# An attention stage whose block-mean rows are made in place by a product and a ScalarE copy

## The chip, the cores and the metric

One core of a Trainium2 chip runs the kernel. The metric is the device time of one execution in microseconds (us); the number to move is the median of several runs. The engines are named as in the profile: PE is TensorE, ACT is ScalarE, DVE is VectorE, POOL is GpSimd, SP is SyncE, whose queue issues nearly all transfers here.

## What is computed

Attention over 2 x 8 heads of 768 positions and 64 dimensions, and behind it two dense gated layers. Every query sees its neighbours within 15 positions and 24 rows that each stand for a block of 32 keys: the block's maximum on the key side, the block's mean on the value side.

```python
nb = S // block                                             # 768 // 32 = 24
k_sum = k.reshape(B, H, nb, block, D).max(axis=3)
v_sum = v.reshape(B, H, nb, block, D).mean(axis=3)
scores_l = scale * np.matmul(q, k.transpose(0, 1, 3, 2))    # kept where |i - j| < 16
scores_s = scale * np.einsum('bhsd,bhnd->bhsn', q, k_sum) + np.log(block)
a = softmax(np.concatenate([scores_l_m, scores_s], axis=-1))
out = np.matmul(a, np.concatenate([v, v_sum], axis=2))
# then: h = x @ w_in; x = (h * cos(h)) @ w_out; and once more with h * tanh(softplus(h))
```

## The kernel before

The attention runs over 8 pairs of heads. A pair has six tiles of 128 queries, so there are 48 steps, numbered 0 to 47: step i is tile i mod 6 of pair i // 6. Everything is in float32.

A step is one pass of the loop at the end of `attention`. It handles several tiles at once, at different stages: the scores of tile i (`scores`), the exponentials of tile i - 1 (`softmax1`), the normalising of tile i - 3 (`softmax2`), the transposes of the probabilities of tile i - 5 (`probsT`) and the product with the values of tile i - 6 (`pv`). The work is collected in lists by phase (`at`), and `flush` issues them in the order of `ORDER`. So on PE a step reads: two score products (`bank<-kx,qt`), three transposes of probabilities (`bank<-ident,pn`), the preparation of a later pair (transposes `ident,kn` or `ident,qn`), and the product of probabilities and values, in two parts: `pt,vn` for the 128 positions of the tile itself, then `pt,vt` for the tail. The accumulators of `pv` are banks 6 and 7 in turn, two steps each. After each flush `filler` adds the early work on the dense layers' weights (L106 the load, L130 and L172/L174 on ACT, L135, L144 and L179 on DVE).

The tail tile `vt` holds, for each of the six tiles of a pair, the rows that are not in the tile: 15 neighbour rows on each side and the 24 block means, for two heads, 108 rows in all. Three such tiles rotate (`VT[n % 3]`). The neighbour rows are loaded from DRAM by `load_v`. The block means come in two ways:

- Pairs 0 to 2: PE makes them from the values by a product with `means` (`prep_vm`, in step 6n + 3, for pair 0 in step 4), ACT copies them to the tile `vm`, and `prep_vs` has SP send them to their rows of `vt` by two transfers, each repeated over the six tiles.
- Pairs 3 to 7: POOL adds up the 32 rows of each block in `vb` in nine instructions (`block_sums`, steps 14 to 21 and 26 to 33), scales the sum into `vs` (120 partitions, one for each block of five heads), and `prep_vs` sends 24 partitions for each head to `vt`.

On POOL a step's own work is the normalising: one instruction for the tile's own 128 columns, and for the tail one of 108 columns where the tile is even and two of 60 and 48 columns where it is odd. SP works its queue in order: a transfer that waits, for its source or for room, holds up all behind it.

## Time and profile before

| | us |
|---|---|
| median of 3 runs (617.55 to 620.34) | 619.26 |
| the profiled execution | 620.15 |
| its span, first to last instruction | 618.4 |
| PE busy in the span | 605.7 |
| ACT, DVE, POOL busy | 393.8, 457.6, 173.5 |
| mean granted TensorE clock | 0.992 of full |

The rows further down come from the same execution. A timeline row gives the start, the time from the first start to the last end, the engine, the line, the operation with output and inputs, and the count of instructions; in brackets stand the idle time ahead of it and what ended that. A matmul in float32 is two instructions, so "x4" is two products. [...]

### The profile page before, as it was taken

What the parts mean: (1) busy time and instruction counts of PE and PEld (TensorE: products, weight loads), DVE (VectorE), ACT (ScalarE), POOL (GpSimd) and SP (SyncE); (2) the same over time, 40 slices, a digit from 0 to 9 for tenths busy, and PEclk for the clock granted to TensorE, in tenths of its full rate; (3) what the DMA queues carried; (4) which work ended last, traced back from release to release, by engine and by line L of the source; (5) the groups of instructions that cost most, each with busy time, mean ns of one, the idle gap of its engine ahead of it and who ended that gap; (6) DMA issues with size and microseconds to landing.
All of it is one profiled execution on the core that took longest, in us unless ns stands there. A gap on an engine that the chain in (4) does not pass through costs nothing.

```text
span 618.4 us, 9241 instructions
## 1 busy us (share of the span) xinstructions
PE 605.7 (98%) x3212; PEld 505.9 (82%) x3212; DVE 457.6 (74%) x952; ACT 393.8 (64%) x849; POOL 173.5 (28%) x261
## 2 busy tenths in 40 slices
PE   8989899999999999999999999999999999999998
PEld 4768688888888788888888878888888888888886
DVE  6638677488767786868686898977878786968544
ACT  6749789786558777766767769765454545444331
POOL 6538846653612542323232470000000000000000
PEclk9979999999999999999999999999999999999999
DMA  8886941302012212212211221142221222221004
GB/s 185 165 201 148 205 120 40 103 1 69 1 36 100 71 68 69 70 68 69 68 69 69 69 69 33 36 137 68 69 68 69 69 68 103 68 69 36 0 35 170
DMA packets 58842, 49.90 MB, mean 81 GB/s; under 512 B 44396, under 2 KB 44652, under 8 KB 58796
## 3 DMA queue, kind: packets, MB, share of 16 engines
q1 hardware_dynamic: 57708, 49.06, 27.2%
q8 instruction: 25, 0.41, 0.3%
q10 hardware_dynamic: 1088, 0.26, 0.2%
q14 instruction: 21, 0.17, 0.1%
HBM read 45.57 MB, written 3.15 MB: 79 GB/s over the span
## 4 chain that ended last, share of the span: by engine, by line
PE 92%; DMA 3%; DVE 2%; POOL 1%; SPq 1%; issue 1%; ACT 0%; ACTq 0%; POOLq 0%
PE bank L729 33%; PE bank L920 21%; PE bank L907 14%; PE bank L285 13%; PE bank L213 5%; PE bank L621 5%; DMA vt<-vs 1%; DMA qn<-in_q_dram 1%; POOL wx L193 1%; DVE gl L628 1%; POOL pn L285 1%; DVE acc L628 0%; DMA kn<-in_k_dram 0%; DMA vt<-vm 0%; DVE ws L179 0%
## 5 line engine op out<-in xcount | busy, mean ns | idle before, releaser
L729 PE MATMUL bank<-xh,ws 128*128 128x512 f32 (+1 forms) x464 | 133.5, 345 | 0.0
L920 PE MATMUL bank<-ws,gh 128*128 128x512 f32 (+1 forms) x388 | 119.2, 389 | 0.0
L628 DVE TENSOR_TENSOR acc<-acc,bank 128x512 f32<-128x512 f32 (+1 forms) x133 | 90.0, 681 | 35.0 <-PE bank L920 25.9
L907 PE MATMUL bank<-gh,ws 128*128 128x512 f32 x288 | 95.7, 390 | 0.0
L729 PEld LDWEIGHTS bank<-xh,ws 128*128 128x128 f32 x464 | 83.3, 189 | 12.2
L920 PEld LDWEIGHTS bank<-ws,gh 128*128 128x128 f32 x388 | 70.9, 188 | 13.0
L729 PE MATMUL bank<-xl,ws 128*128 128x512 f32 (+1 forms) x232 | 80.1, 345 | 0.0
L920 PE MATMUL bank<-ws,gl 128*128 128x512 f32 (+1 forms) x194 | 75.0, 387 | 0.0
L907 PEld LDWEIGHTS bank<-gh,ws 128*128 128x128 f32 x288 | 54.2, 188 | 10.8
L628 DVE TENSOR_TENSOR gl<-gg,gh 128x512 fp32r<-128x512 f32 x78 | 56.3, 735 | 8.4 <-ACT gh L882 8.0
L285 POOL TENSOR_TENSOR pn<-pb,rs 128x256 f32<-128x256 f32 (+3 forms) x120 | 51.5, 452 | 38.9 <-DVE rs L285 14.7
L172 ACT CAST ws<-wx 128x512 fp32r<-128x512 f32 (+1 forms) x62 | 36.3, 597 | 39.7 <-DVE wx L156 20.7
L882 ACT CAST gh<-gg 128x512 fp32r<-128x512 f32 x96 | 58.3, 618 | 3.2 <-DVE gg L874 2.2
L729 PE MATMUL bank<-ws,ws 128*128 128x512 f32 (+1 forms) x300 | 56.9, 338 | 0.3 <-DVE ws L179 0.3
L907 PE MATMUL bank<-gl,ws 128*128 128x512 f32 x144 | 56.4, 392 | 0.1
L729 PEld LDWEIGHTS bank<-ws,ws 128*128 128x128 f32 x300 | 48.1, 189 | 7.8 <-DVE ws L179 0.7
L285 DVE CUSTOM_DVE_ANT_0 pb<-bank,mask 128x182 f32<-128x182 f32 x96 | 29.5, 344 | 28.9 <-PE bank L285 23.2
L729 PEld LDWEIGHTS bank<-xl,ws 128*128 128x128 f32 x232 | 43.8, 189 | 6.7
L867 DVE SCALAR_TENSOR_TENSOR gg<-gg,bank 128x512 f32<-128x512 int32 x36 | 24.2, 684 | 27.2 <-ACT gg L864 27.2
L920 PEld LDWEIGHTS bank<-ws,gl 128*128 128x128 f32 x194 | 36.4, 188 | 7.7
L285 ACT ACTIVATE pb<-pb,mx 128x182 f32<-128x182 f32 x96 | 42.4, 449 | 0.2 <-DVE mx L285 0.2
L628 POOL TENSOR_TENSOR gl<-gg,gh 128x512 fp32r<-128x512 f32 x18 | 24.1, 1336 | 62.3 <-ACT gh L882 60.0
(146 smaller groups left out, 1188.2 us busy)
## 6 DMA issues: line engine op xcount, KB each, us to landing
wst<-in_moe_w_in_dram SPq DMA_DIRECT2D x32, 512.0 KB, 3.6
wst<-in_moe_w_out_dram SPq DMA_DIRECT2D x32, 512.0 KB, 3.3
vn<-in_v_dram SPq DMA_DIRECT2D x16, 192.0 KB, 3.7
out_dram<-acc SPq DMA_DIRECT2D x11, 256.0 KB, 2.0
kn<-in_k_dram SPq DMA_DIRECT2D x14, 192.0 KB, 3.8
qn<-in_q_dram SPq DMA_DIRECT2D x14, 192.0 KB, 4.2
vb<-in_v_dram SPq DMA_DIRECT2D x4, 480.0 KB
vt<-in_v_dram SPq DMA_DIRECT2D x32, 18.8 KB, 3.1
```

What stands on the lines that cost most here:

```text
L172: nc.scalar.copy(hi, x)
L193: (nc.vector if l else nc.gpsimd).tensor_tensor(out=z, in0=u, in1=v, op=op)
L213: nc.tensor.matmul(ps, lhsT=SLOT[4 * (g % 2) + a][:, 512 * c + 128 * f:512 * c + 128 * f + 128], rhs=X[e][:, c, TB * j:TB * j + TB], start ...
L285: todo[phase].append(lambda: fn(*a, **kw))
L621: nc.tensor.matmul(ps, lhsT=x, rhs=y, start=(n == 0), stop=(n == len(mm) - 1))
L628: (eng or nc.vector).tensor_tensor(out=out, in0=x, in1=y, op=op)
L729: nc.tensor.matmul(ps, lhsT=u, rhs=v, start=start and n == 0, stop=stop and n == len(mm) - 1, skip_group_check=True)
L867: nc.vector.scalar_tensor_tensor(out=x["r"], in0=x["r"].bitcast(I32), scalar=-1.0, in1=src(), op0=ALU.mult, op1=ALU.add)
L882: nc.scalar.copy(slot[0], x["r"])
L907: nc.tensor.matmul(BANK[bank], lhsT=x, rhs=y, start=(n == 0 and (h == HF or not stay)), stop=(n == len(mm) - 1 and (h == NH - 1 or not stay)))
L920: nc.tensor.matmul(BANK[bank][:, 0:d1 - d0], lhsT=x, rhs=y, start=(n == 0 and (h == 0 or not stay)), stop=(n == len(mm) - 1 and (h == NH - ...
```

## The change

`vt` gets another order of rows: 32 for the means of the first head (24 used), 32 for the second, then the four groups of 15 neighbour rows, 124 in all. `prep_vm` now makes the means of a pair at these partitions in PSUM for all pairs: for pairs 0 to 2 by the product with `means`, which has 64 columns now, for pairs 3 to 7 by one product (two for pair 5) with a selection matrix `pick` from the block sums; the factor 1/32 is in `pick`. Two ACT copies (`spread`) write the rows straight from PSUM into the six tiles, one for each head: one at the end of step 6n + 3, one at the start of step 6n + 4. `vm`, the transfers `vt<-vm` and `vt<-vs` and the scaling on POOL are gone. The block sums start two steps earlier (steps 12 to 19 and 24 to 31). The normalised tiles `pn` are four fixed tiles, and the tail is normalised by two instructions in every step.

```diff
-            BLOCKS = {a + c: [(g, c)] for g, a in ((0, 14), (1, 26)) for c in range(7)}
+            BLOCKS = {a + c: [(g, c)] for g, a in ((0, 12), (1, 24)) for c in range(7)}
...
+            def build_pick():
+                nc.gpsimd.memset(pick, 0.0)
+                nc.gpsimd.affine_select(
+                    out=pick, in_=pick, pattern=[[-NB, HPG + 2], [-1, MROW]], compare_op=ALU.not_equal,
+                    fill=1.0 / BLK, base=NB, channel_multiplier=1)
+                nc.gpsimd.memset(pick[:, :, NB:MROW], 0.0)
...
-                at("misc", nc.gpsimd.tensor_tensor, out=x[:, r:r + n, :], in0=x[:, r:r + n, :],
-                   in1=x[:, r + w:r + w + n, :], op=ALU.add)
-                if c == 8:
-                    at("misc", nc.gpsimd.tensor_scalar, out=VS[g], in0=x[:, 0, :], scalar1=1.0 / BLK, scalar2=None,
-                       op0=ALU.mult)
+                at("misc", nc.gpsimd.tensor_tensor, out=x[:, r:r + n, :] if c < 8 else VS[g][:, None, :],
+                   in0=x[:, r:r + n, :], in1=x[:, r + w:r + w + n, :], op=ALU.add)
...
-                ps = BANK[6 if n == 1 else 7][0:NB, 0:128]
...
-                vm = VM[n] = p2.tile([NB, 2 * D], F32, tag="vm", name="vm")
-                at("ev", nc.scalar.copy, vm, ps)
-
-            def prep_vs(n):
...
-                    at("misc", nc.sync.dma_start, out=VT[n % 3][r0:r0 + NB, :, e, :],
-                       in_=x[:, None, :].to_broadcast([NB, NTILE, D]))
+                ps = BANK[6 if n % 2 else 7][0:2 * MROW, 0:128]
+                if 2 * n < MADE:
+                    for t in range(NTILE):
+                        at(phase, nc.tensor.matmul, ps, lhsT=means[:, t].rearrange("p e j -> p (e j)"),
+                           rhs=VN[n % 3][:, t, 0:3:2, :], start=(t == 0), stop=(t == NTILE - 1))
+                else:
+                    ps = ps[:, 0:D]
+                    g, c = divmod(2 * n - MADE, HPG)
+                    mm = [(g, c + 1)] + [(g + 1, 0)] * (c == HPG - 1)
+                    for m, (g, c) in enumerate(mm):
+                        at(phase, nc.tensor.matmul, ps, lhsT=pick[:, c:c + 2].rearrange("p e j -> p (e j)"), rhs=VS[g],
+                           start=(m == 0), stop=(m == len(mm) - 1))
+                VM[n] = ps if 2 * n < MADE else None, ps
+
+            def spread(n, e, phase):
+                made, ps = VM[n]
+                x = ps[MROW * e:MROW * e + MROW, D * e if made is not None else 0:][:, 0:D]
+                at(phase, nc.scalar.copy, VT[n % 3][MROW * e:MROW * e + MROW, :, e, :],
+                   x[:, None, :].to_broadcast([MROW, NTILE, D]))
...
-                9: [lambda n: prep_vm(n), lambda n: prep_vs(n)],
+                9: [lambda n: prep_vm(n), lambda n: spread(n, 0, "misc")],
+                10: [lambda n: spread(n, 1, "xh")],
...
-                if STEPS[i][1] % 2 == 0:
-                    norm(0, SIDE, SIDE, 0, 128 + SIDE)
-                else:
-                    norm(0, REST - HALO, HALO, 0, EXT - HALO)
-                    norm(SIDE, -GAP, GAP, HALO, 128 + GAP)
+                odd = STEPS[i][1] % 2
+                norm(2 * MROW, 2 * HALO, HALO, HALO, 0, EXT - HALO)
+                norm(GAP * odd, MROW, -GAP if odd else GAP, GAP, HALO, 128 + GAP)
```

What follows are rows of the instruction order of the two kernels, in which a name ends with a running number. On SP, ahead of the first weight load of the dense layers (`wst`), before:

```order
L319 DMA vt_113<-in_v_dram 15x5x64
L298 DMA qn<-in_q_dram 128x6x64 x2
L285 DMA vt_112<-vm 24x6x64 x2
L298 DMA kn<-in_k_dram 128x6x64 x2
L106 DMA wst<-in_moe_w_in_dram 128x512
```

and now:

```order
L327 DMA vt_113<-in_v_dram 15x5x64
L330 DMA vt_113<-in_v_dram 15x5x64
L309 DMA qn<-in_q_dram 128x6x64 x2
L309 DMA kn<-in_k_dram 128x6x64 x2
L106 DMA wst<-in_moe_w_in_dram 128x512
```

The two transfers with the means of pair 1 are gone from between the loads; nothing else moved on this queue.

On ACT, steps 27 and 28 (pair 4), before; `pt` is the copy of transposed probabilities that ends a step, `ws` is weight work:

```order
L285 COPY pt_1020<-bank5_63 128x384
L174 ACTIVATE ws0_85<-wx_929 128x512
L285 CAST xh_93<-bank6_64 128x256
L285 ACTIVATE pb_1023,sm_1022<-pb_1023,mx_1024 128x182 x2
L285 COPY pt_1051<-bank5_63 128x384
```

and now:

```order
L296 COPY pt_1017<-bank5_63 128x384
L296 COPY vt1_112<-bank7_65 32x6x64
L174 ACTIVATE ws0_85<-wx_927 128x512
L296 COPY vt1_112<-bank7_65 32x6x64
L296 CAST xh_93<-bank6_64 128x256
L296 ACTIVATE pb_1020,sm_1019<-pb_1020,mx_1021 128x182 x2
L296 COPY pt_1048<-bank5_63 128x384
```

The two copies into `vt` stand on both sides of the weight work, ahead of the exponentials of step 28.

On PE, steps 21 and 22 (pair 3), from the last transposes of probabilities in step 21 to the value product of step 22, before, with what an instruction waits for in brackets:

```order
L285 MATMUL bank5_63<-ident_116,pn_770 108x128 [waits Pool_49]
L285 MATMUL bank4_62<-ident_116,qn_542 128x128 [waits DMAHW2_49,DMAHW1_49]
L285 MATMUL bank4_62<-ident_116,qn_542 128x128
L285 MATMUL bank7_65<-pt_800,vn2_110 128x128 x2
L285 MATMUL bank7_65<-pt_800,vt2_113 128x128
...
L285 MATMUL bank6_64<-pt_832,vn2_110 128x128 x2
L285 MATMUL bank6_64<-pt_832,vt2_113 128x128
```

and now:

```order
L296 MATMUL bank5_63<-ident_116,pn0_120 124x128 [waits Pool_49]
L296 MATMUL bank6_64<-vs0_114,pick_119 64x64 [waits DVE_49,Pool_49]
L296 MATMUL bank4_62<-ident_116,qn_548 128x128 [waits DMAHW6_49,DMAHW5_49]
L296 MATMUL bank4_62<-ident_116,qn_548 128x128
L296 MATMUL bank7_65<-pt_802,vn2_110 128x128 x2
L296 MATMUL bank7_65<-pt_802,vt2_113 128x128
...
L296 MATMUL bank6_64<-pt_832,vn2_110 128x128 [waits Activation_49]
L296 MATMUL bank6_64<-pt_832,vn2_110 128x128
L296 MATMUL bank6_64<-pt_832,vt2_113 128x128
```

The new product waits for POOL (the sums in `vs`) and writes bank 6, which the value product of step 22 takes next; that one now waits for ACT, for the second copy out of that bank.

## Rows read from the trace of the kernel before

**Rows 1.** Timeline of PE, steps 11 to 17, the `pt,vt` products alone.
```profile
27.74 0.39 PE L285 MATMUL bank<-pt,vt 108*128 108x128 f32 x2
...
33.49 0.77 PE L285 MATMUL bank<-pt,vt 108*128 108x128 f32 x2 [3.71 <-DMA vt<-vm]
...
39.77 0.39 PE L285 MATMUL bank<-pt,vt 108*128 108x128 f32 x2
...
45.09 0.39 PE L285 MATMUL bank<-pt,vt 108*128 108x128 f32 x2
...
46.97 0.39 PE L285 MATMUL bank<-pt,vt 108*128 108x128 f32 x2
```

**Rows 2.** Timeline of PE: q transposes of step 21, `pt,vt` of steps 23 and 25.
```profile
53.80 0.38 PE L285 MATMUL bank<-ident,qn 128*128 128x128 f32 x2
...
58.22 0.39 PE L285 MATMUL bank<-pt,vt 108*128 108x128 f32 x2
...
62.41 0.39 PE L285 MATMUL bank<-pt,vt 108*128 108x128 f32 x2
```

**Rows 3.** Timeline of PE, `pt,vt` of steps 29, 30 and 32.
```profile
69.91 0.39 PE L285 MATMUL bank<-pt,vt 108*128 108x128 f32 x2
...
74.86 0.46 PE L285 MATMUL bank<-pt,vt 108*128 108x128 f32 x2 [2.92 <-DMA vt<-vs]
...
80.24 0.39 PE L285 MATMUL bank<-pt,vt 108*128 108x128 f32 x2
```

**Rows 4.** Windows: behind the two waits, six steps from 18, the dense layers.
```profile
33.49:39.77 6.28, 6.28 (x30) 5.03 (x31) 1.97 (x11) 2.24 (x8) 0.00 (x0) 0.57 1.00 244
74.86:80.24 5.38, 5.38 (x30) 4.42 (x31) 2.43 (x12) 2.31 (x9) 2.23 (x5) 0.68 0.91 235
47.29:58.54 11.25, 11.25 (x92) 9.28 (x91) 9.36 (x43) 10.53 (x39) 9.76 (x23) 1.00 0.69 164
200.00:618.00 418.00, 414.93 (x2067) 352.40 (x2065) 319.65 (x520) 248.74 (x443) 67.11 (x57) 1.00 0.21 70
```

**Rows 5.** Timeline of SP's queue: issues around the first wait.
```profile
30.31 1.69 SPq L285 DMA_DIRECT2D vt<-vm  x2
...
33.20 0.54 SPq L106 DMA_DIRECT2D wst<-in_moe_w_in_dram  x1
```

**Rows 6.** Timeline of PE, step 15: the product with `means`.
```profile
41.08 1.49 PE L285 MATMUL bank<-vn,means 128*24 128x128 f32 x12
```

**Rows 7.** Groups by form, ACT, 0 to 108 us (count, busy us, mean ns, idle before).
```profile
L285 ACT COPY pt<-bank 128x384 f32<-128x384 f32 x43 | 20.6, 479 | 3.4 <-PE bank L285 3.0
```

**Rows 8.** Timeline of ACT, end of step 45 and start of step 46.
```profile
103.56 0.48 ACT L285 COPY pt<-bank 128x384 f32<-128x384 f32 x1 [0.23 <-PE bank L285]
103.94 0.62 ACT L172 CAST ws<-wx 128x512 fp32r<-128x512 f32 x1
104.45 0.38 ACT L285 CAST xh<-bank 128x256 fp32r<-128x256 f32 x1
```

**Rows 9.** Timeline of PE, step 46: the value product.
```profile
104.96 0.61 PE L285 MATMUL bank<-pt,vn 128*128 128x128 f32 x4
```

**Rows 10.** Groups by form, POOL, 0 to 115 us: normalising of the tail.
```profile
L285 POOL TENSOR_TENSOR pn<-pb,rs 128x108 f32<-128x108 f32 x24 | 8.9, 369 | 0.0
L285 POOL TENSOR_TENSOR pn<-pb,rs 128x60 f32<-128x60 f32 x24 | 8.3, 344 | 0.0
L285 POOL TENSOR_TENSOR pn<-pb,rs 128x48 f32<-128x48 f32 x24 | 6.6, 273 | 1.9
```

**Rows 11.** Timeline of POOL: scaling of the first sums, two instructions of the second.
```profile
55.98 0.37 POOL L285 TENSOR_SCALAR vs<-vb 120x64 f32<-120x64 f32 x1
...
68.26 0.72 POOL L285 TENSOR_TENSOR vb<-vb 120x256 f32<-120x256 f32 x1
...
70.29 1.18 POOL L285 TENSOR_TENSOR vb<-vb 120x256 f32<-120x256 f32 x1
```

**Rows 12.** Timeline of DVE, step 14: first touch of the first weight load.
```profile
39.96 0.42 DVE L135 TENSOR_SCALAR wst<-wst 128x512 int32<-128x512 int32 x1
```

More of the change, by code (lines that the diff above doesn't have):

```diff
@@ L218 @@
     HPG = 5
+    MROW = 32
+    TAIL = 2 * MROW + 4 * HALO
     MADE = B * H - 2 * HPG
@@ L234, in attention @@
             mask = p1.tile([128, 3, EXT], F32, tag="mask", name="mask")
-            means = p1.tile([128, NTILE, NB], F32, tag="means", name="means")
+            means = p1.tile([128, NTILE, 2, MROW], F32, tag="means", name="means")
+            pick = p1.tile([HPG * NB, HPG + 2, MROW], F32, tag="pick", name="pick")
+            PN = [p1.tile([128, 256 + TAIL], F32, tag=f"pn{i}", name=f"pn{i}") for i in range(4)]
             def build_consts():
@@ L337, in block_sums @@
                            (0, 2, 2), (0, 1, 1))[c]
-                at("misc", nc.gpsimd.tensor_tensor, out=x[:, r:r + n, :], in0=x[:, r:r + n, :],
-                   in1=x[:, r + w:r + w + n, :], op=ALU.add)
-                if c == 8:
-                    at("misc", nc.gpsimd.tensor_scalar, out=VS[g], in0=x[:, 0, :], scalar1=1.0 / BLK, scalar2=None,
-                       op0=ALU.mult)
-            def prep_vm(n, phase="tr"):
-                if 2 * n >= MADE:
-                    return
-                ps = BANK[6 if n == 1 else 7][0:NB, 0:128]
-                for t in range(NTILE):
-                    at(phase, nc.tensor.matmul, ps, lhsT=means[:, t, :], rhs=VN[n % 3][:, t, 0:3:2, :],
-                       start=(t == 0), stop=(t == NTILE - 1))
-                vm = VM[n] = p2.tile([NB, 2 * D], F32, tag="vm", name="vm")
-                at("ev", nc.scalar.copy, vm, ps)
@@ L377, in init_v @@
                     nc.vector.memset(x, 0.0)
+                for x in PN:
+                    nc.vector.memset(x[:, 256:256 + 2 * MROW].rearrange("p (e j) -> p e j", e=2)[:, :, NB:MROW], 0.0)
             def turned(n, src, c, x=None):
@@ L424, in attention @@
                 1: [lambda n: prep_q(n, 2)],
-                4: [lambda n: prep_vm(n, "tp"), lambda n: prep_vs(n)],
+                4: [lambda n: prep_vm(n, "tp"), lambda n: spread(n, 0, "ev"), lambda n: spread(n, 1, "ev")],
             }
@@ L433, in attention @@
                 6: [lambda n: prep_q(n, 2, BANK[7])],
-                9: [lambda n: prep_vm(n), lambda n: prep_vs(n)],
-            }
-            BLOCKS = {a + c: [(g, c)] for g, a in ((0, 14), (1, 26)) for c in range(7)}
-            BLOCKS.update({a + 7: [(g, 7), (g, 8)] for g, a in ((0, 14), (1, 26))})
+                9: [lambda n: prep_vm(n), lambda n: spread(n, 0, "misc")],
+                10: [lambda n: spread(n, 1, "xh")],
+            }
+            BLOCKS = {a + c: [(g, c)] for g, a in ((0, 12), (1, 24)) for c in range(7)}
+            BLOCKS.update({a + 7: [(g, 7), (g, 8)] for g, a in ((0, 12), (1, 24))})
             def asked(i):
@@ L500, in softmax2, with norm @@
                 pb, rs = PB.pop(i), SM["rs", i // 2][:, 2 * (i % 2):2 * (i % 2) + 2]
-                pn = PB[i] = p3.tile([128, 2 * EXT], F32, tag="pn", name="pn")
+                pn = PB[i] = PN[i % 4]
                 at("norm", nc.gpsimd.tensor_tensor, out=pn[:, 0:256].rearrange("p (e j) -> p e j", e=2),
                    in0=pb[:, :, SIDE:SIDE + 128], in1=rs[:, :, None].to_broadcast([128, 2, 128]), op=ALU.mult)
-                def norm(o, step, w, a, d):
+                def norm(o, pair, step, w, a, d):
                     at("norm", nc.gpsimd.tensor_tensor,
-                       out=bass.AP(pn.tensor, pn.offset + 256 + o, [pn.ap[0], [REST, 2], [step, 2], [1, w]]),
+                       out=bass.AP(pn.tensor, pn.offset + 256 + o, [pn.ap[0], [pair, 2], [step, 2], [1, w]]),
                        in0=bass.AP(pb.tensor, pb.offset + a, [pb.ap[0], [EXT, 2], [d, 2], [1, w]]),
                        in1=rs[:, :, None, None].to_broadcast([128, 2, 2, w]), op=ALU.mult)
-                if STEPS[i][1] % 2 == 0:
-                    norm(0, SIDE, SIDE, 0, 128 + SIDE)
-                else:
-                    norm(0, REST - HALO, HALO, 0, EXT - HALO)
-                    norm(SIDE, -GAP, GAP, HALO, 128 + GAP)
+                odd = STEPS[i][1] % 2
+                norm(2 * MROW, 2 * HALO, HALO, HALO, 0, EXT - HALO)
+                norm(GAP * odd, MROW, -GAP if odd else GAP, GAP, HALO, 128 + GAP)
             def probsT(i):
```

21 lines of the change are left out of this document (8 added, 13 removed).

## Prediction

> **What bounds the kernel now.** I read the window view first, because it tells which engine has no room in which stretch. In the dense layers PE is busy 414.93 of 418 us [rows 4], so nothing is to be had there, and work that the attention finishes earlier is time off the end. In a clean stretch of the attention (six steps, 47.29 to 58.54) PE is busy the whole 11.25 us; ACT follows with 10.53 and POOL with 9.76 [rows 4]. So a step that waits for nothing takes what PE takes: 46.97 - 45.09 = 1.88 us [rows 1]. Then I looked in PE's timeline for idle time in brackets. There are two large gaps, both ahead of a `pt,vt` product, which needs the tail tile: 3.71 us until `vt<-vm` has landed, in step 12, the first step of pair 1 [rows 1], and 2.92 us until `vt<-vs` has landed, in step 30, the first step of pair 4 [rows 3].
>
> The gaps cost more than they show. [...] So I measure the loss as time between `pt,vt` products against clean steps. Steps 11 to 14: 39.77 - 27.74 = 12.03, less 3 x 1.88, **6.39 us** lost [rows 1]. Steps 29 to 32: 80.24 - 69.91 = 10.33, less 5.64, **4.69 us** [rows 3]. Steps 23 to 25, where the first rows from POOL's sums come in: 62.41 - 58.22 = 4.19, less 3.76, **0.43 us** [rows 2]. Together 11.51 us.
>
> **Part by part.** *The transfers.* SP issued those of pair 1 at 30.31 us [rows 5], behind six loads of values and more, although their source had long been made; PE went on at 33.49 [rows 1], 3.2 us after the issue. With copies the place in SP's queue no longer matters. The neighbour rows and values for the same products were issued ahead of `vt<-vm` in the same queue, so no transfer that PE needs there is later. I take all three losses as gone: **-11.51 us**, the clock's part included, since I find no other gap of PE there that would lower it.
>
> *Products on PE.* Pairs 0 to 2 keep theirs; a product with 64 columns instead of 24 still streams 128 columns. New are six products with `pick`, twelve instructions. The row nearest is the product with `means`: 1.49 us for twelve instructions of 128 streamed columns, 0.124 us each [rows 6]; `pick` streams 64. Between half of that and all of it: 0.7 to 1.5 us, all on the path because PE is. I take 0.9. The transposes of the tail and `pt,vt` stream 128 columns as before; at nothing.
>
> *Copies on ACT.* Two for each pair, 384 elements on each of 32 partitions. The nearest row is the copy of `pt`, 128 x 384 from PSUM, 0.48 us [rows 7]; it holds the engine 103.94 - 103.56 = 0.38 us [rows 8]. Six pieces that repeat the same source have no row; I take 0.38. The three copies of `vm` fall away. ACT had 10.53 us of work in 11.25 [rows 4]; now 10.53 + 0.76 = 11.29 in 11.25 + 0.12. That just fits, with nothing left over. ACT's work trails PE by a share of a step, and what it delivers late (`pt` for the next `pt,vn`) has about a step's room, so I charge 0 to 0.3 us for each of seven pairs, take 0.1 for six, **0.6 us**; the upper end is 2.1.
>
> *A new wait on PE.* The means of pair n lie in the bank that the value product of step 6n + 4 takes, and that product has to wait for the second copy. Behind it in PE's queue stand `pt,vt` and the next step's scores, so all waits. Worst is pair 7 (steps 45 and 46), where no transposes of a later pair lengthen the steps. There the copy of `pt` ends its turn at 103.94; a copy of 0.38, the weight work of 104.45 - 103.94 = 0.51, and a second copy of 0.48 end at 105.31 [rows 8]; the product started at 104.96 [rows 9], and is 0.12 later through `pick`: 0.23 us late. In pairs 3 to 6 a transpose of 0.2 us stands ahead of the product and the step is longer, so they come out even. **0.25 us**, at most 0.2 each for the seven pairs, 1.5. [...]
>
> *POOL.* An even tile's tail takes 344 + 273 ns in place of 369 [rows 10]: 0.25 us more in every second step, 0.74 in six. In the clean six steps POOL then has 9.76 + 0.74 = 10.5 of 11.37 us. It has room, but where the block sums run it has nearly none. What depends on it: the sums of pair 3 were scaled at 55.98 + 0.37 = 56.35 in step 21 [rows 11]; two steps (3.75 us) earlier is 52.60, and the product with `pick` stands where the q transposes of step 21 started, 53.80 [rows 2]. That is 1.2 us of room; eight steps of 0.12 take 1.0 of it, and the scaling that falls away gives 0.37 back. So about 0.6 is left, for the first sums as for the second. I charge 0.2, bounds 0 and 1.0. The larger `means` and `pick` are built on POOL where it waits for others; at nothing, and a few tenths if that is wrong.
>
> *Loads that PE meets sooner.* DVE first touches the weights at 39.96, in step 14 [rows 12]; with 6.4 us gone it comes there at 33.6. The load was issued at 33.20 [rows 5]. The issues of pair 1's transfers took 1.69 us [rows 5], those of pair 0 ahead of it about the same, so the load goes out near 29.8, and with the 3.2 us of the transfer above it lands at 33.0. Just in time; 0.2, and 0 to 1.1.
>
> Sum: -11.51 + 0.9 + 0.6 + 0.25 + 0.2 + 0.2 = **-9.4 us**; with the bounds -10.8 to -4.3. The profiled execution took 620.15 us, 0.9 above the median of 619.26. From 620.15 it would be 610.8, and as a median **609.9 us**; a measurement of this kernel tells about 0.5%, 3.1 us, from no change.
>
> **The rivals.** *POOL comes late.* An addition of block sums took 0.72 us at one place and 1.18 at another [rows 11], so some steps cost POOL 0.46 more. Three of these in one run of sums make 1.4 us, 0.8 over the room; PE would wait for `vs` in steps 21 and 33, 0.8 us each, and longer with a slower clock behind it: 1.6 to 4 us given back, about 612.5. For it: the 9.76 of 11.25. Against it: such steps are few. [...] *Loads take the place.* If the first weight load goes out at 33.20 as before, it lands near 36.4, 2.8 us after DVE asks. PE would stop a little later for the scores, and pay for the clock again: 3 to 5 us given back, about 613.5. *The stalls only change their releaser.* If the second copy ends 1.2 us after PE wants the bank, in each of seven pairs, 8.4 us go back, about 618: no change. That needs ACT to run a step late in all pairs, and the rows show it idle for PE just there (0.23 us ahead of `pt` [rows 8]). *ACT becomes the bound: slower.* If a copy that repeats its source holds ACT for s us, a pair costs 10.53 + 2s against PE's 11.37. Up to s = 0.42 this is free; from s = 1.13 the 7 x (2s - 0.84) us eat the 10 us that the rest gains, and at s = 1.5 they make 15.1 us: 624.4, slower than before. Only a copy more than three times as costly as `pt`'s of equal length does that; no row is near it.
>
> **How the numbers follow.** Forecast (609.9, between 608.4 and 612): 0.67. POOL late (612.5): 0.13. Loads late (613.5): 0.08. Waits that change place (618): 0.07. ACT as the bound (624.4): 0.05. The range from 607.2 (the best sum less the spread of the runs) to 614.9 (all terms at their bad end) takes in the first three, 0.88. Faster by over 0.5%, under 616.2: these 0.88. Within: 0.07. Slower: 0.05.
>
> **What would show it.** In the profile after: no idle time of PE ahead of `pt,vt` above 0.3 us; the clock at 1.00 from 30 to 100 us, where two stretches were below 0.7; the start of the dense layers some 9 to 10 us earlier and all behind it shifted by as much. `vt<-bank` on ACT at 0.4 to 0.5 us confirms the copy's price. Idle time of PE ahead of the product with `pick` would be POOL's; ahead of `pt,vn` in steps 6n + 4 ACT's; ahead of scores near 34 us the weight load's. I am wrong if the transposes, not the tail, were what PE would have waited for next, or if PE's steps lengthen evenly, which would be ACT.

## The result and the profile after

| | before | after |
|---|---|---|
| median of 7 runs, us | 619.56 (617.55 to 622.01) | 612.05 (611.85 to 616.30) |
| the profiled execution, its span | 620.15, 618.4 | 613.37, 611.7 |
| first product of the dense layers | 108.45 | 101.68 |
| PE, from the start of step 7 to that of step 47 | 88.62 | 79.74 |

The time is 0.9886 of the one before (95% interval 0.9858 to 0.9915): 7.5 us less, where 9.4 were forecast. Of most kernels here one run or more is about 4 us longer than the rest (one such was profiled, and it had lost 4.3 us before step 5); the medians are over all runs, and where such runs are half of them the lower group stands beside.

The page of the kernel after, engines and granted clock in 40 slices of the span:

```profile
PE 604.6 (99%) x3224; PEld 504.6 (82%) x3224; DVE 458.4 (75%) x956; ACT 400.3 (65%) x862; POOL 177.2 (29%) x286
...
PEclk9999999999999999999999999999999999999999
```

No slice is below 9; before, the granted clock read 0.57 and 0.68 of full speed in the stretches behind the two waits [rows 4]. In the timeline of PE these are the `pt,vt` products of steps 11, 12, 14, 29, 30 and 32, which answer to [rows 1, 3]:

```profile
29.57 0.39 PE L296 MATMUL bank<-pt,vt 124*128 124x128 f32 x2
31.45 0.39 PE L296 MATMUL bank<-pt,vt 124*128 124x128 f32 x2
...
35.20 0.39 PE L296 MATMUL bank<-pt,vt 124*128 124x128 f32 x2
...
65.92 0.39 PE L296 MATMUL bank<-pt,vt 124*128 124x128 f32 x2
67.79 0.39 PE L296 MATMUL bank<-pt,vt 124*128 124x128 f32 x2
...
71.55 0.39 PE L296 MATMUL bank<-pt,vt 124*128 124x128 f32 x2
```

None carries a bracket. Steps 11 to 14 and 29 to 32 take 5.63 us each, three times 1.88; before they took 12.03 and 10.33. So the stalls are gone whole, and the 2 us that are missing from the forecast lie in what replaced the transfers. Three places show in the trace.

First, a step with a product of `pick`. PE, step 21:

```profile
48.38 0.58 PE L296 MATMUL bank<-kx,qt 64*128 64x182 f32 x4
48.89 0.55 PE L296 MATMUL bank<-ident,pn 128*128 128x128 f32 x3
49.37 0.33 PE L296 MATMUL bank<-vs,pick 120*64 120x64 f32 x2
49.63 0.44 PE L296 MATMUL bank<-ident,qn 128*128 128x128 f32 x2
...
50.66 0.58 PE L296 MATMUL bank<-kx,qt 64*128 64x182 f32 x4
```

From one score product to the next it is 2.28 us, 0.40 more than 1.88. The product holds PE's queue 0.26 us (49.37 to 49.63), and it begins 0.48 us behind the start of the transposes of the probabilities, where the next product of a step without `pick` begins 0.38 behind it.

Second, the start. In step 6 PE stood idle 0.96 us. PE, then POOL, then ACT:

```profile
17.35 0.52 PE L296 MATMUL bank<-ident,pn 128*128 128x128 f32 x3 [0.96 <-POOL pn L296]
```

```profile
11.95 2.11 POOL L296 TENSOR_TENSOR pn<-pb,rs 128x256 f32<-128x256 f32 x6 [2.73 <-DVE rs L296]
```

```profile
14.76 0.94 ACT L296 COPY vt<-bank 32x384 f32<-32x384 f32 x2
15.73 0.45 ACT L296 ACTIVATE pb<-pb,mx 128x182 f32<-128x182 f32 x1
...
16.73 0.48 ACT L296 COPY pt<-bank 128x384 f32<-128x384 f32 x1
```

The bracket names POOL, but POOL had made that `pn` by 14.06. What PE really lacked is the bank that ACT empties with `pt`, at 17.2; ACT was late with it because the two copies of pair 0 (`vt<-bank`) stand ahead of exponentials, and `pt` behind them.

Third, ACT. Its copies take what was forecast (0.47 us mean), but a pair now takes ACT nearly all of the time. The window of pair 4 (behind its length stand the busy time and the count of PE, PEld, DVE, ACT and POOL, as in [rows 4], then the granted clock as a share of full speed, the busy share of the DMA engines, and GB/s; PEld is PE's loading of the stationary side), and the last pair, where PE waits for ACT:

```profile
54.49:66.23 11.74, 11.70 (x93) 9.45 (x92) 10.22 (x45) 11.38 (x41) 9.65 (x22) 1.00 0.77 178
```

```profile
99.50 0.52 PE L296 MATMUL bank<-ident,pn 128*128 128x128 f32 x3 [0.27 <-ACT pt L296]
```

### The profile page after: what moved, and what is told of

Its sections match the earlier page's. It is cut to its first block, busy times and chain, and to the rows that moved or that the text cites. A ratio compares the mean times of both kernels' runs of the same rounds, so it can differ in the third digit from the quotient of the medians.

```text
span 611.7 us, 9308 instructions
## 1 busy us (share of the span) xinstructions
PE 604.6 (99%) x3224; PEld 504.6 (82%) x3224; DVE 458.4 (75%) x956; ACT 400.3 (65%) x862; POOL 177.2 (29%) x286
## 4 chain that ended last, share of the span: by engine, by line
PE 95%; DVE 2%; ACT 1%; POOL 1%; DMA 1%; issue 0%; ACTq 0%; POOLq 0%
PE bank L740 33%; PE bank L931 21%; PE bank L296 15%; PE bank L918 14%; PE bank L213 5%; PE bank L632 5%; POOL wx L193 1%; DMA kn<-in_k_dram 1%; DVE gl L639 1%; DVE acc L639 0%; ACT pb L296 0%; DVE ws L179 0%; DVE gg L885 0%; POOL pn L296 0%; ACT pt L296 0%
## 5 line engine op out<-in xcount | busy, mean ns | idle before, releaser
L296 POOL TENSOR_TENSOR pn<-pb,rs 128x256 f32<-128x256 f32 x144 | 55.0, 414 | 26.5 <-DVE rs L296 15.1
```

The costliest lines, as they stand in the source:

```text
L296: todo[phase].append(lambda: fn(*a, **kw))
```

## Experiments

Two measures go beside the time of each, both from the starts of the steps' score products in the profiled run: how long PE took from step 5 to step 7 (the start) and from step 7 to step 47 (the rest of the attention but for its last step).

| kernel | median us | step 5 to 7 | step 7 to 47 |
|---|---|---|---|
| before | 619.56 | 3.73 | 88.62 |
| before without transfers | 608.08 | 3.39 | 77.06 |
| before, transfers on ACT's queue | 624.32 | 6.09 | 87.83 |
| after without copies | 610.41 | 3.39 | 79.36 |
| after | 612.05 | 4.30 | 79.74 |
| first copies later | 611.54 | 3.72 | 79.86 |
| pick in halves | 612.33 | 4.30 | 79.99 |
| pick wide | 614.21 (lower three 611.96 to 612.14) | 4.30 | 79.72 |
| copies twice | 617.83 | 4.26 | 85.48 |
| sums one step later | 613.28 | 4.30 | 80.69 |
| pick wide, copies by VectorE | 613.63 (lower three 610.58 to 612.24) | 3.72 | 79.28 |
| sums by 32 partitions, first form | 613.83 | 3.72 | 83.71 |
| the same, second form | 612.35 | 3.72 | 82.01 |
| the same, third form | 608.80 | 3.72 | 77.34 |

### What the stalls cost, and what replaced them

```diff
-                    at("misc", nc.sync.dma_start, out=VT[n % 3][r0:r0 + NB, :, e, :],
-                       in_=x[:, None, :].to_broadcast([NB, NTILE, D]))
```

> The kernel before, with the sixteen transfers that put the rows of means into the tail tiles left out (these rows stay zero in the output's computation); all else, the products of means, the copies of vm and POOL's sums too, stands. My theory: the three waits of PE ahead of the tail product and the low clock behind them, 11.5 us, go whole and nothing takes their place: 619.56 - 11.5 = 608.0 (607.5 to 609), dense layers from about 97 us, no wait of PE above 0.3 us between 20 and 97 us, granted clock 1.00 there. The difference to the changed kernel (612.05) is then the price of what it puts in place of the transfers, 4.0 us. Rival: what came late behind the waits (weight loads, POOL's sums) takes part of the gain: PE waits elsewhere and the time is 610 to 612, and the new products and copies cost next to nothing.

Measured: 608.08 us. No wait of PE is left between 12 us and the dense layers. Between steps 7 and 47 it gives 88.62 - 77.06 = 11.56 us; the forecast had put 11.51 on the three stalls. So nothing took their place, and the price of the replacement is 612.05 - 608.08 = 4.0 us, where the prediction had 2.15.

The other half, the changed kernel without its copies:

```diff
             def spread(n, e, phase):
...
-                at(phase, nc.scalar.copy, VT[n % 3][MROW * e:MROW * e + MROW, :, e, :],
-                   x[:, None, :].to_broadcast([MROW, NTILE, D]))
+                return
```

> The changed kernel without ScalarE's copies into the tail tiles (their rows of means stay zero); the products with pick, the new order of the tail and its normalising on POOL stand. My theory: the copies cost the changed kernel 1.0 us at the start (those of pair 0 stand ahead of the exponentials of step 4, and PE stood idle 0.96 us in step 6), 0.4 us in pair 7 and 0.2 us elsewhere: 612.05 - 1.6 = 610.4 (610.0 to 610.8), and step 6 has no idle time of PE. What is left over the kernel before without its transfers, 2.2 us, is then the products with pick. Rival: the copies are free (as the sum of the prediction nearly had them, 0.85 us for copies and bank wait): 611.2 or more, and the loss at the start stays, since it is the late landing of the first loads.

Measured: 610.41 us. So the 4.0 us split into 1.64 for the copies and 2.33 for the rest. The trace puts nearly all of that rest on the products with `pick`: 79.36 - 77.06 = 2.30 us between steps 7 and 47, of which the five steps with `pick` make 2.20 (2.29 us for the plain ones).

### The place in SP's queue

```diff
-                    at("misc", nc.sync.dma_start, out=VT[n % 3][r0:r0 + NB, :, e, :],
+                    at("misc", nc.scalar.dma_start, out=VT[n % 3][r0:r0 + NB, :, e, :],
```

> The kernel before with one thing changed: the sixteen transfers of the rows of means are issued on ScalarE's queue instead of SP's, right behind the copy of vm in program order. My theory: the place in SP's queue was the cause of the three waits. Issued in step 9 instead of 30.31 us, the rows lie in the tiles long before step 12, so PE's waits ahead of pt,vt are gone and the clock stays at 1.00 there. What the issues hold of ScalarE is not known; on SP two took 1.69 us, and if they hold ScalarE as long, a pair costs it 10.53 + 1.69 = 12.2 us against PE's 11.3, and PE waits for ScalarE instead: between 608 (issues free) and 614 (6 x 0.9 us more). For the transfers of pairs 3 to 7 ScalarE also waits for POOL's sums. Rival: the transfers themselves are slow, whoever issues them: PE waits ahead of pt,vt in step 12 and 30 as before, 618 or more.

Measured: 624.32 us, slower than before (1.008, 1.005 to 1.011). No wait ahead of `pt,vt` is left, so the transfers are in time when SP's other loads don't stand ahead of them: the place in the queue was the cause of the two long waits. It was not that of the 0.43 us of pair 3. In the kernel before, SP issued those transfers as soon as POOL's sums were there, at 56.35:

```profile
56.38 1.70 SPq L285 DMA_DIRECT2D vt<-vs  x2
```

The time goes elsewhere. ACT's queue, and PE in step 23:

```profile
27.25 1.67 ACTq L285 DMA_DIRECT2D vt<-vm  x2
```

```profile
58.25 0.52 PE L285 MATMUL bank<-ident,pn 128*128 128x128 f32 x3 [3.07 <-ACT pt L285]
```

Two issues hold ACT 1.67 us, as long as they held SP (1.69), and for pairs 3 and 5 they wait for POOL's sums, with the exponentials behind them: PE then waits 3.07 and 2.24 us for `pt`. Between steps 7 and 47 the kernel is still 0.8 us ahead of the one before; it loses 2.4 us at the start and 1.3 behind step 47. The upper end of the expectation, 614, counted the issues alone. Two copies of 0.47 us do the same work in little over half of ACT's time.

### The copies of pair 0

```diff
-                4: [lambda n: prep_vm(n, "tp"), lambda n: spread(n, 0, "ev"), lambda n: spread(n, 1, "ev")],
+                4: [lambda n: prep_vm(n, "tp")],
+                5: [lambda n: spread(n, 0, "misc"), lambda n: spread(n, 1, "misc")],
```

> The changed kernel with one thing moved: the two copies of pair 0 stand one step later, behind the copy of pt in step 5 and no longer ahead of the exponentials of step 4. My theory: the idle 0.96 us of PE in step 6 is theirs, so step 7 comes 0.9 us earlier against step 5 (3.4 us behind it instead of 4.30), and the time is 611.1. Rival: the loss at the start is the late first load of the profiled run alone, which varies from run to run: 612.05, and PE waits in step 6 as before. A third way: the copies now hold up the value product of step 6, which needs them: 612 or more, with a wait of PE ahead of pt,vt in step 6.

Measured: 611.54 us. ACT, then PE:

```profile
14.35 0.48 ACT L296 COPY pt<-bank 128x384 f32<-128x384 f32 x1
14.72 0.95 ACT L296 COPY vt<-bank 32x384 f32<-32x384 f32 x2
15.70 0.45 ACT L296 ACTIVATE pb<-pb,mx 128x182 f32<-128x182 f32 x1
```

```profile
15.72 0.44 PE L296 MATMUL bank<-ident,qn 128*128 128x128 f32 x2 [0.21 <-ACT vt L296]
```

`pt` is copied first, the idle 0.96 us is gone, and the start falls from 4.30 to 3.72 us: 0.58, and 0.51 in the time. It is less than the 0.9 expected: 0.33 us stay against the kernel without copies (3.39), and the one wait that the trace shows there is that of a transpose for bank 7, which the copies now hold (0.21 us).

### What a product with `pick` costs

First each product in two halves of 32 columns:

```diff
-                    for m, (g, c) in enumerate(mm):
-                        at(phase, nc.tensor.matmul, ps, lhsT=pick[:, c:c + 2].rearrange("p e j -> p (e j)"), rhs=VS[g],
-                           start=(m == 0), stop=(m == len(mm) - 1))
+                    for d in range(0, D, D // 2):
+                        for m, (g, c) in enumerate(mm):
+                            at(phase, nc.tensor.matmul, ps[:, d:d + D // 2],
+                               lhsT=pick[:, c:c + 2].rearrange("p e j -> p (e j)"), rhs=VS[g][:, d:d + D // 2],
+                               start=(m == 0), stop=(m == len(mm) - 1))
```

> The changed kernel with each of the six products with pick made in two of 32 columns instead of one of 64; the same rows come out. It asks what sets their price: a step with such a product took 0.40 us more than one without (2.28 against 1.88), where 0.15 was forecast. My theory: an instruction costs about 0.13 us however few columns it streams, so twelve more instructions add 12 x 0.13 = 1.6 us: 613.6, steps with pick at 2.54 us, the pair with two sums at 2.9. Rival: the price goes by columns, as the prediction had it for its lower end, and the 0.14 us around the product are a single switch: the time stays at 612.05 and the steps at 2.28.

Measured: 612.33 us; a step with `pick` takes 2.37 us. Two more instructions add 0.09 us, not 0.26: my theory of a fixed price for each instruction fell. In the changed kernel the second product of pair 5 adds 0.12 us. So of the 0.40 us about 0.12 are the two instructions, as the lower bound of the prediction had it, and 0.28 stand around them once for each step with `pick`, whether it has one product or two. Then the stationary side 128 columns wide, with the same 64 streamed:

```diff
-            pick = p1.tile([HPG * NB, HPG + 2, MROW], F32, tag="pick", name="pick")
+            pick = p1.tile([HPG * NB, HPG + 4, MROW], F32, tag="pick", name="pick")
...
-                    ps = ps[:, 0:D]
+                    ps = BANK[6 if n % 2 else 7][:, 0:D]
...
-                           lhsT=pick[:, c:c + 2].rearrange("p e j -> p (e j)"), rhs=VS[g],
+                           lhsT=pick[:, c:c + 4].rearrange("p e j -> p (e j)"), rhs=VS[g],
```

> The changed kernel with pick widened: each of the six products uses 128 columns of it instead of 64 as its stationary side and writes 128 partitions, of which the copies take the same ones as before. It streams the same 64 columns. It asks where the 0.28 us around the product come from: splitting it in two halves added only 0.09 us to a step, and the second product of pair 5 0.12, so of the 0.40 us that a step with pick takes more, about 0.12 are the two instructions themselves. In the changed kernel the weight load of pick starts only with its product (49.37), 0.17 us of idle time behind the load before it, and so does the next one (49.63). Theory: that is the change of the stationary side's width, from 128 to 64 columns and back; with 128 the loads run ahead, a step with pick takes about 2.05 us instead of 2.28, and the time is 612.05 - 6 x 0.23 = 610.7. Rival: it is the wait for POOL and for the bank that an instruction carries, or the 64 streamed columns; then the steps stay at 2.28 and the time at 612.05.

The weight loads (PEld) of step 21, first after, then with the wide `pick`, and there PE's rows too:

```profile
48.89 0.31 PEld L296 LDWEIGHTS bank<-ident,pn 128*128 128x128 f32 x3 [0.21 <-issue]
49.37 0.19 PEld L296 LDWEIGHTS bank<-vs,pick 120*64 120x64 f32 x2 [0.17 <-POOL pn L296]
49.63 0.20 PEld L296 LDWEIGHTS bank<-ident,qn 128*128 128x128 f32 x2
```

```profile
47.60 0.31 PEld L296 LDWEIGHTS bank<-ident,pn 128*128 128x128 f32 x3 [0.21 <-issue]
47.88 0.30 PEld L296 LDWEIGHTS bank<-vs,pick 120*128 120x128 f32 x2
48.05 0.26 PEld L296 LDWEIGHTS bank<-ident,qn 128*128 128x128 f32 x2
```

```profile
47.99 0.33 PE L296 MATMUL bank<-vs,pick 120*128 120x64 f32 x2
48.16 0.39 PE L296 MATMUL bank<-ident,qn 128*128 128x128 f32 x2
```

With 64 columns each load starts only with its product (49.37, 49.63), with 128 it starts 0.11 us ahead (47.88 for 47.99, 48.05 for 48.16). The step takes 2.05 us, 0.23 less, as the theory had it, though the product waits for the same sums: the change of width and back costs that, and 0.05 of the 0.40 us stay unexplained. What happens in PE at such a change no trace here shows. The transposes behind the score products, whose stationary side has 64 rows, look alike in both kernels (load and product both start at 48.89 after, at 47.60 and 47.61 with the wide `pick`); what that costs was not tried.

The time, though, did not fall: the lower runs stand at 612.0, and steps 7 to 47 take 79.72 us against 79.74. Pair 6 in this kernel:

```profile
76.70:88.44 11.74, 11.47 (x93) 9.46 (x92) 9.34 (x44) 11.37 (x41) 6.89 (x19) 1.00 0.32 87
```

PE's work is 0.24 us shorter than the 11.71 it had, and the pair still takes 11.74. The halves point the same way: there a step with `pick` is 0.09 us longer, and yet pair 4 takes only 0.02 us more than in the changed kernel (11.76). Something else sets the pace.

### Whether ACT is the bound

Each copy made twice in pairs 1 to 7:

```diff
-                at(phase, nc.scalar.copy, VT[n % 3][MROW * e:MROW * e + MROW, :, e, :],
-                   x[:, None, :].to_broadcast([MROW, NTILE, D]))
+                for _ in range(2 if n else 1):
+                    at(phase, nc.scalar.copy, VT[n % 3][MROW * e:MROW * e + MROW, :, e, :],
+                       x[:, None, :].to_broadcast([MROW, NTILE, D]))
```

> The changed kernel with each copy into a tail tile made twice for pairs 1 to 7, so that a pair costs ScalarE 0.94 us more. It tests how much room ScalarE and the bank have. My theory: ScalarE has about 0.3 us left in six steps of pairs 3 to 6 (busy 11.34 of 11.70 between 53.0 and 64.7 us), more in pairs 1 and 2; PE then waits some 0.6 us for each of four pairs and 0.9 in pair 7: 612.05 + 3.3 = 615.4 (614 to 617), with PE's waits labelled ACT ahead of the transposes of probabilities or of the value product. Rival, by the prediction's threshold (7 x (2s - 0.84) with s = 0.94 in place of 0.47): 612.05 + 6.6 = 618.6. Second rival, the copies are hidden wherever they stand: 612.5 at most.

Measured: 617.83 us, 5.8 more than after. PE's waits, and the window of pair 5:

```profile
64.47 0.71 PE L296 MATMUL bank<-pt,vn 128*128 128x128 f32 x4 [0.50 <-ACT vt L296]
66.19 0.52 PE L296 MATMUL bank<-ident,pn 128*128 128x128 f32 x3 [0.27 <-ACT pt L296]
```

```profile
67.53:80.27 12.74, 12.08 (x95) 9.59 (x94) 10.63 (x44) 12.31 (x43) 9.56 (x23) 1.00 0.42 110
```

Pair 5 takes 12.74 us instead of 11.78: the whole 0.94 of ACT's added work. Pairs 3, 4, 6 and 7 lose 1.0 us each, pairs 1 and 2 only 0.4. The 0.3 us that ACT seems to have left in a pair (11.38 of 11.74) are no room for the copies: they lie ahead of them, most in one wait for a bank of PE's. ACT in the changed kernel, pair 4:

```profile
57.68 0.37 ACT L296 COPY kx<-bank 128x256 f32<-128x256 f32 x1 [0.23 <-PE bank L296]
```

Between 61.27 us, ahead of the first copy, and the end of the pair ACT has no gap above 0.02 us. My own expectation took them for room and was 2.4 us too low; the prediction's threshold, which counts all of it against PE, was 0.8 too high. The first wait (step 28) is the bank wait that the prediction priced at 0.25 us for one copy.

The check from the other side, with the wide `pick` and VectorE making the copies of pairs 1 to 7:

```diff
-                at(phase, nc.scalar.copy, VT[n % 3][MROW * e:MROW * e + MROW, :, e, :],
+                at(phase, nc.vector.tensor_copy if n else nc.scalar.copy, VT[n % 3][MROW * e:MROW * e + MROW, :, e, :],
```

> The version with the first copies moved (611.54), with pick 128 columns wide, and with the copies into the tail tiles of pairs 1 to 7 made by VectorE instead of ScalarE, at the same places. With the wide pick alone a step with pick took 2.05 us instead of 2.28, but the time from step 7 to 47 stayed (79.72 us against 79.74), and PE waited 0.27 us twice for ScalarE's pt. Theory: ScalarE had become the bound, a pair takes it 11.74 us, just what the wide pick should have gone below; freed of the copies, a pair takes what PE needs, 11.66 - 0.23 = 11.43 us, and the time is 611.54 - 6 x 0.23 - 0.4 (ScalarE's waits of pair 7) = 609.8 (609.3 to 610.5). Rival: the wide pick's gain went elsewhere (PE's own order, POOL), and the time stays at 611.5. Second rival: VectorE, at 10.05 of 11.78 us, is delayed by the copies, and the scores with it: over 611.5, with waits of PE labelled DVE.

Measured: 613.63 us, with a lower group of 610.58 to 612.24. The windows of pairs 4 and 6:

```profile
56.73:68.62 11.89, 11.76 (x94) 9.47 (x93) 11.05 (x45) 10.87 (x39) 10.22 (x23) 1.00 0.89 184
...
80.49:91.93 11.44, 11.44 (x93) 9.47 (x92) 10.15 (x46) 10.64 (x39) 6.78 (x19) 1.00 0.36 89
```

Pair 6 takes 11.44 us, PE's work alone, as the theory had it (11.43). So ACT was what held the wide `pick`'s gain; whether by the sum of its work or by the place of the two copies in it, neither run tells apart. In pair 4 VectorE has 11.05 of 11.89 us, its two copies take 1.10 us in a row, and it comes late with the queries' copies (one ends at 67.52, and PE's next transposes of queries start at 67.58); the second rival holds there, though no wait of PE is labelled so. Over all steps the trace gives 79.86 - 79.28 = 0.58 us, not the 1.7 expected.

### POOL's room

```diff
-            BLOCKS = {a + c: [(g, c)] for g, a in ((0, 12), (1, 24)) for c in range(7)}
+            BLOCKS = {a + c: [(g, c)] for g, a in ((0, 13), (1, 25)) for c in range(7)}
...
```

> The changed kernel with POOL's sums of both groups one step (1.88 us) later, 13 and 25 instead of 12 and 24 (the kernel before had 14 and 26). In the changed kernel the sums ended at 47.98 and 71.99 us, and PE came to their first product at 49.37 and 72.85: 1.39 and 0.86 us of room. My theory: PE now waits for POOL ahead of pick, about 0.5 us in step 20 or 21 and 1.0 us in step 32 or 33, and loses that or, with a lower clock behind it, up to twice that: 613.5 to 615. This is the rival 'POOL late' of the prediction brought about. Rival: POOL catches up by itself since its room was larger than the rows show, and nothing changes: 612.05.

Measured: 613.28 us, 1.2 more and just under the expected range. PE:

```profile
48.26 0.33 PE L296 MATMUL bank<-vs,pick 120*64 120x64 f32 x2 [0.22 <-POOL vs L296]
...
72.52 0.33 PE L296 MATMUL bank<-vs,pick 120*64 120x64 f32 x2 [0.52 <-POOL vs L296]
```

One step later and PE waits for POOL, 0.74 us in all; at 12 and 24 it does not. So the changed kernel's room was less than a step, but some 0.3 and 0.5 us larger than the rows show: the waits are 0.22 and 0.52 us, where 0.5 and 1.0 were expected.

### A version without `pick`

With ACT and `pick` known, a layout that needs neither: POOL adds heads whose blocks lie at partitions 0, 32, 64 and 96, and VectorE copies the rows straight from `vs`, scaled by 1/32; the first copies stand later, as above.

```diff
+                for e in (2 * m, 2 * m + 1):
+                    r0, rows = NB * (MADE + HPG * g + e), MROW if e < HPG - 1 else NB
+                    nc.sync.dma_start(out=VB[g][MROW * e:MROW * e + rows], in_=src[r0:r0 + rows])
...
+                x = VS[g][MROW * c:MROW * c + NB, None, :].to_broadcast([NB, NTILE, D])
+                y = VT[n % 3][MROW * e:MROW * e + NB, :, e, :]
...
+                    at("misc", nc.vector.tensor_scalar, out=y, in0=x, scalar1=1.0 / BLK, scalar2=None, op0=ALU.mult)
```

> A version built on what the runs show: the first copies moved as in the experiment on them (611.54), and the products with pick gone. POOL's sums are made for three groups of four heads (pairs 2 to 7) instead of two of five (pairs 3 to 7), with a head's blocks loaded at partitions 0, 32, 64 and 96, so that they lie where a copy can take them; VectorE copies them (scaled) straight from POOL's result into the tail tiles, with no product, no bank and no work of ScalarE. Theory: -2.2 us of pick products, -1.5 of the product with means of pair 2, -0.4 of waits for ScalarE in pair 7: 611.54 - 4.1 = 607.4 (606.8 to 608.5). Rival: POOL, which now has 27 such additions instead of 18, or the additional loads make PE wait: 609 to 612, with PE's idle time labelled POOL or DMA. Second rival: VectorE, busy 9.66 of 11.70 us, is slowed by copies of 384 elements that repeat their source and delays the scores: a wait labelled DVE.

Measured: 613.83 us. The rival, with a size that I had not thought of. POOL, then PE:

```profile
28.67 0.72 POOL L289 TENSOR_TENSOR vb<-vb 120x256 f32<-120x256 f32 x1 [10.09 <-DMA vb<-in_v_dram]
```

```profile
30.01 0.94 PE L289 MATMUL bank<-ident,pn 128*128 128x128 f32 x3 [4.98 <-POOL pn L289]
```

The first addition, asked of POOL in step 7, waits 10 us for its load, and the normalising behind it in POOL's queue with it. In the second form the first group starts at step 12 again, pair 2 gets its product back, the groups have four, four and two heads, and VectorE's copies stand one step later:

```diff
+    HEADS = (4, 4, 2)
...
-            STARTS = ((0, 7), (1, 19), (2, 31))
+            STARTS = ((0, 12), (1, 24), (2, 36))
```

> The version with POOL's sums laid out by 32 partitions and copied by VectorE once more, with the cause of its loss taken away: there POOL's first addition stood in step 7 and waited until 28.67 us for the load, 10 us, and the normalising behind it with it, so PE stood idle 4.98 us. Now the first group starts at step 12 as in the changed kernel, which is late enough for it (and for pair 3 only, so the means of pair 2 come from a product again): three groups of four, four and two heads at steps 12, 24 and 36, loads of the second and third at 20 and 32. Theory: against the version with the first copies moved (611.54), the pick products (2.25 us) and ScalarE's waits of pair 7 (0.45) fall away: 608.8 (608.2 to 609.5), near the kernel before without any transfers (608.08). Rival: 27 additions of POOL instead of 18, at places where it has 10.55 us of work in 11.80, or loads that land late, make PE wait for pn again: 610 to 613.

Measured: 612.35 us, inside the rival's range. The first wait is gone, the same one came at the second group. POOL, then SP:

```profile
60.56 0.72 POOL L290 TENSOR_TENSOR vb<-vb 120x256 f32<-120x256 f32 x1 [5.33 <-DMA vb<-in_v_dram]
```

```profile
47.33 0.79 SPq L337 DMA_DIRECT2D vb<-in_v_dram  x2
...
49.24 1.40 SPq L337 DMA_DIRECT2D vb<-in_v_dram  x2
```

The loads could only go out when the first sums had given `vb` free, and landed 10 us behind their second issue. The third form asks for them in halves, the upper half of a group while the lower half of the one before is still being added; the third group's sums start at step 34, and `means` is used 128 columns wide:

```diff
-                for e in range(k // 2 * m, k // 2 * m + k // 2):
+                half = slice(0, 16) if m else slice(16, 32)
+                for e in range(k):
...
-                r, w, n = ((0, 16, 4), (4, 16, 4), (8, 16, 4), (12, 16, 4), (0, 8, 4), (4, 8, 4), (0, 4, 4),
+                r, w, n = ((16, 8, 4), (20, 8, 4), (16, 4, 4), (12, 4, 4), (0, 8, 4), (4, 8, 4), (0, 4, 4),
...
-            STARTS = ((0, 12), (1, 24), (2, 36))
+            STARTS = ((0, 12), (1, 24), (2, 34))
...
-                     20: ["b10"], 21: ["b11"], 32: ["b20"], 33: ["b21"]}.get(i, [])
+                     18: ["b10"], 21: ["b11"], 30: ["b20"], 33: ["b21"]}.get(i, [])
...
-                        at(phase, nc.tensor.matmul, ps, lhsT=means[:, t].rearrange("p e j -> p (e j)"),
+                        at(phase, nc.tensor.matmul, ps, lhsT=means[:, t:t + 2].rearrange("p t e j -> p (t e j)"),
```

> The version with sums laid out by 32 partitions, its loads mended: in the run before, POOL waited 5.33 us for the second group's load, whose issue had to wait for the first group's sums (47.3 us) and which landed at 60.5; PE stood idle 2.38 us and lost 4.27 us with the low clock behind it. Now the loads come in two halves of 16 rows, the sums begin with the upper half and give it back after the fourth addition, so that the next group's upper half is asked for in step 18 instead of 20; the third group starts at step 34, since POOL with one addition per step (1.08 + 0.73 us) is longer than a step of pair 7 (1.66). And means is 128 columns wide as a stationary side, like pick in the run with the wide pick, where that let the weight loads run ahead. Theory: from step 7 to step 47 PE took 82.01 us there against 79.86 in the version with the first copies moved (611.54); without the 4.27 it is 77.74, so 609.4, and 0.24 less for each of the three products with means: 608.7 (608.2 to 609.4). Rival: the loads land late all the same, since the transfers are busy with weights there, and POOL makes PE wait: 610 to 613.

Measured: 608.80 us (0.982 of before, 0.977 to 0.986), 0.1 from the theory and 3.2 below the changed kernel. From 16 us to the dense layers the trace names one wait of PE, in pair 7, for POOL:

```profile
91.46 0.52 PE L290 MATMUL bank<-ident,pn 128*128 128x128 f32 x3 [0.26 <-POOL pn L290]
```

That step and the one ahead of it take 1.96 and 1.92 us, where a step of pair 7 takes 1.66. A step with `means` takes 3.22 us instead of 3.48, 0.26 less: the change of width once more. A pair takes PE what it took in a clean stretch of the kernel before [rows 4]:

```profile
51.54:62.79 11.25, 11.25 (x91) 9.28 (x91) 10.24 (x41) 10.54 (x39) 10.19 (x21) 1.00 1.01 194
```

## Why the prediction was right

**The stalls** carried it. 11.51 us were read off the gaps as time between `pt,vt` products, with the stretch of low clock (0.57 of full speed in 6.28 us behind the first wait, 0.68 in 5.38 us behind the second [rows 4]); the kernel without transfers gave 11.56 between steps 7 and 47, and its clock, a mean of 0.992 before, read 0.999. That the place in SP's queue was the cause of the two long ones is shown by the other queue: no wait ahead of `pt,vt` is left there, though the time went to ACT.

**The sum was 1.9 us too good**, all in the costs: 4.0 us measured for 2.15. Products and copies were put 2.2 us too low; POOL and the loads, 0.4 us too high, hid some of it by luck.

- *Products with `pick`*: 0.9 forecast (0.7 to 1.5), 2.3 measured, outside the bounds. The instructions themselves came at the lower bound, 0.06 us each. What was mis-sized is what stands around them, 0.28 us in each of the five steps, of which 0.23 come from the change of the stationary side's width. The row that the price was taken from [rows 6] could not show this, because it groups twelve instructions of one width.
- *Copies*: 0.6 and 0.25 for the bank wait forecast, 1.64 measured. A copy's 0.47 us were right, and 0.38 between steps 7 and 47 with 0.3 behind them are near the forecast. The rest, 0.91, is the start: pair 0 got no term, though its copies, too, stand ahead of exponentials. Moving those two alone gave back 0.51.
- *POOL*: 0.2 forecast, no wait measured. The sums ended 1.39 and 0.86 us ahead of their products, where 0.6 was left in the forecast:

```profile
47.66 0.32 POOL L296 TENSOR_TENSOR vs<-vb 120x64 f32<-120x64 f32 x1
...
71.67 0.32 POOL L296 TENSOR_TENSOR vs<-vb 120x64 f32<-120x64 f32 x1
```

- *Loads met sooner*: 0.2 forecast, none measured. The first weight load went out at 29.33 (29.8 forecast), and DVE asked for it only at 35.56.

```profile
29.33 0.55 SPq L106 DMA_DIRECT2D wst<-in_moe_w_in_dram  x1
```

**The rivals.** POOL late and loads late did not come; POOL came late as soon as its sums were moved by one step, at 1.2 us. By the time alone 612.05 lies nearer to "POOL late" (612.5) than to 609.9, and just outside the forecast's 608.4 to 612; that PE has no wait for `vs` is what rules it out. The bank wait is real, but one copy ends in time except in pair 7, step 46 of the changed kernel:

```profile
97.26 0.47 ACT L296 COPY vt<-bank 32x384 f32<-32x384 f32 x1
```

```profile
97.79 0.71 PE L296 MATMUL bank<-pt,vn 128*128 128x128 f32 x4
```

The product starts when the copy has ended, and the step takes 1.81 us, 0.15 more than without copies, where 0.23 were forecast. With two copies the wait is 0.38 to 0.50 us in pairs 3 to 6 and 0.89 in pair 7. ACT as the bound was put at 0.05 for a slower result, and rightly, since that needed 1.13 us a copy. In a milder form it holds: "that just fits, with nothing left over" was so exact that in pairs 3, 4 and 6 ACT sets the pace: 11.74 us, where PE takes 11.66 without the copies and is busy 11.47 with the wide `pick`.

**What would show it.** No idle time ahead of `pt,vt`, the clock, and the copies at 0.4 to 0.5 us came as said. The dense layers start 6.8 us earlier, not 9 to 10: besides the terms above, the profiled run began 1.2 us late (step 5 at 14.61 us against 13.38). That is a loss of this one run: with POOL's sums a step later, which changes nothing so early, the profiled run reached step 5 at 13.21.

## What to carry to other kernels

Measure a stall as time between the same instructions of clean steps; the gap in brackets was some 60% of it. When a wait is replaced by work, price the work where the order puts it, the first pair and the last one too: here the waits were sized to 0.1 us, and every error came from the replacement. When two engines need nearly the same time for a pair (here PE 11.66 us, ACT's pace 11.74), making one faster can give nothing: the wide `pick` took 0.24 us of a pair's work from PE, and steps 7 to 47 took 79.72 us for 79.74. The version that won took work from both.

## What had not been expected of the hardware

The product with `pick`, 64 columns wide as a stationary side between products of 128, cost 0.23 us for the change (a step with it took 2.28 us, and 2.05 with `pick` 128 columns wide), nearly twice the 0.12 us of its own two instructions. Writing 64 useless partitions removed that, though it saved time only where PE set the pace: pair 6 went from 11.75 us to 11.74 with ACT's copies, and to 11.44 with VectorE's.

Two transfers of 24 x 384 elements held the issuing engine as long on ACT (1.67 us) as on SP (1.69 and 1.70 us).

VectorE's copy of a head's rows from `vs` took 0.34 us at 43.06 us and 0.91 us at 55.93 us in the first form of the version above; what made the difference was not tried.

The profiled run of the kernel with VectorE's copies reached step 5 at 17.56 us instead of 13.3. Its early products on PE:

```profile
8.90 0.98 PE L296 MATMUL bank<-kx,qt 64*128 64x182 f32 x4
...
14.39 2.65 PE L296 MATMUL bank<-vn,means 128*64 128x128 f32 x12
```

```profile
5.00:17.56 12.56, 12.32 (x52) 7.21 (x50) 4.88 (x26) 6.26 (x25) 5.92 (x19) 1.00 1.10 210
```

Two score products take 0.98 us for 0.58, the twelve instructions of `means` 2.65 for 1.52, and yet the granted clock of that stretch reads 1.00. PE had no gap above 0.24 us there. The changed kernel's own profiled run, 1.2 us late at step 5, shows the same up to 9 us (two score products at 7.31 take 0.98 us; the clock reads 1.00). What held PE is not shown.
